# Stores of 64 rows with two adjacent slots, k features by head then slot, batches 1 and 2 transposed on TensorE, and a new step order, in a linear-attention and gated-convolution kernel

## The chip, the cores and the metric

The kernel runs on one core of one Trainium2 chip. The metric is the device time of the launch in microseconds, as a median over several runs. A profile is one execution of its own; its span runs from the first to the last instruction, and its device time lies a little above its span.

## The reference

For each of 8 batches and 8 heads, 576 positions of 64 features go through a linear attention with cosine weights. Its output, with heads side by side as 576 x 512, goes through a projection to three parts, a circular convolution of the second part along the sequence (by FFT), a product of the three and an output projection. All inputs and the output are float32.

```python
def phi(x, c, s):                       # c, s: cos, sin of pi/2 * pos / S
    r = np.maximum(x, 0.0)
    return np.concatenate([r * c, r * s], axis=-1)
q_p, k_p = phi(q, cos_w, sin_w), phi(k, cos_w, sin_w)
kv = np.einsum('bhsf,bhsd->bhfd', k_p, v)
z = np.sum(k_p, axis=2)
num = np.einsum('bhsf,bhfd->bhsd', q_p, kv)
den = np.einsum('bhsf,bhf->bhs', q_p, z)[..., None] + 1e-06
x = (num / den) with heads side by side             # 8 x 576 x 512
proj = x @ w_proj;  x1, x2, x3 = its three parts of 512
x2_conv = irfft(rfft(x2, axis=1) * rfft(filter_fft, axis=0), axis=1)
out = (x1 * x2_conv * x3) @ w_out
```

## The kernel before, in words

**Layout.** The 576 positions of a batch are 64 partitions x 9 consecutive rows. Rows 0 to 4 of each nine stand on partitions 0 to 63 and rows 5 to 8 on partitions 64 to 127, so that a tile of 128 partitions has five "slots" (NJ = 5); slot t holds row t on the lower and row t + 5 on the upper half, and the fifth slot only row 4. This holds for the inputs (load_rows, L260) and for the output rows.

**A batch.** GpSimd's queue loads q, k and v with a cast to fp16 (step_load, L275, "Lq", "Lk", "Lv"); for the first half (4 heads) of batch 0, k and v come over SP's queue as float32 instead (step_load32, "Sk", "Sv", into k32 and v32). VectorE, or ScalarE where the plan's word ends in 'a, makes the features: relu of k ("pk", step_pk, L594) and of q ("pq", L605), a plain relu of all slots and then one scaled relu a slot. k's features lie in `kp` by slot, then head (L196); q's in `qp` by head, then slot. v is scaled by the cosine ("va", L615), and TensorE sums kv over the slots ("kv", L628). q is transposed ("qt", step_qt, L643): for batches from DMA_QT = 1 on by a DMA transpose of two heads on SP's queue, for batch 0 by ten TensorE transposes and one eviction of 128 x 1280. "num" (L664) multiplies it with kv and divides into `att`. `att` is transposed to `xt`: "xt" (L690) is a DMA transpose on SP's queue of two of the four blocks, "xp" (L698) ten TensorE transposes with an eviction of 128 x 1152; batch 0 has "xp", all others "xt". Then come the gates x1 and x3 ("ga", "gb", L830, and their product "g"), the symmetric folding of the sequence ("bf", L709, on VectorE, in halves or whole), the projection x2 ("pr", L742), the forward transform ("dm", "dr", "dl"), the product with the filter's transform ("pd"), the inverse transform ("inv", L865), the unfolding with the gate ("y", L882) and the output ("out", L914).

**Output.** "out" has three groups a batch: slots 0 and 1, slots 2 and 3, and slot 4. For the first two groups one eviction of 128 x 1024 goes to one of three `os` buffers, and SP issues two stores, one for each slot: 128 partitions to the two groups of 64 rows t and t + 5 of each nine (`ov`, L917 and L956). Slot 4 is evicted on 128 partitions as two halves of the columns and stored as two blocks of 64 rows x 256 (L946). In the last batch each slot is evicted in two halves by VectorE and ScalarE and stored alone, the even ones by SP, the odd ones by ScalarE's queue (L959 to L966).

**The order** is written by hand: PLAN (L21) is a list of words, each the next step of a generator, and run (L984) takes them in turn; every instruction enters its engine's or queue's stream in that order. 'v and 'a send an eviction or a relu to VectorE or ScalarE instead of its usual engine; ~ holds a load until the last VectorE instruction issued so far. UNITS (L15) gives the PSUM unit (of four, two banks each) for each use in turn. Some first words are tables: "io" (iotas on GpSimd), "cols", "rows", "tf", "ti", "th", "zero", "pad", "feo", "h" (filter).

Of the kernel before, what the change touches and what calls it, by code (L numbers as in the profile page):

```python
# [15 lines left out]
    "0123013023021032102032102121203031230212030320321320312032021301301231031203123031023103"  # L16
    "2130130202313021302130213013201201230231203120301320312031023021002310123212013213213023"
    "1031202031030120323123031201032020230213203"
# [3 lines left out]
    io:1 io:0 zero: pd32:1 zero: pad:0 pad:5 cols: pad:4 cols: id: rows: io:2 rows: cols:*2 rows:  # L22
    ~Lq:0.0 rows:*5 pd32:0 Sk:0.0 pk:0.0 pk:0.0'a th: pad:1 Sv:0.0 th:'v Lq:0.1 rows:*2 pk:0.0
    va:0.0'v tf:1'v ones:0 pk:0.0'a va:0.0 va:0.0'v*2 pk:0.0'a pk:0.0 warm:0.12 pq:0.0 tf:0'v
    pq:0.0 va:0.0 ones:1 kv:0.0 pq:0.0'a tf:0 pq:0.1 kv:0.0 tf:0 Lv:0.1 Lk:0.1 tf:0 id: pq:0.0
    pq:0.0'a*2 Lv:1.2 qt:0.0 pq:0.1'a*3 th:'v*2 va:0.1'v th: qt:0.1*2 pq:0.1*2 qt:0.2*2 qt:0.0'v
    va:0.1'v pk:0.1 va:0.1 num:0.0 pk:0.1*2 pad:3 io:3 rows: Lw:2.0.4 ~Lw:0.0.4 qt:0.3*2 tf:0
    ~Lk:1.2 pk:0.1 num:0.1 pk:0.1 num:0.1 num:0.0 num:0.1 num:0.0 pk:0.1 pad:2 va:0.1'v*2 Lw:1.0.4
    num:0.1 tf:1 Lq:1.2 kv:0.1*2 num:0.0 num:0.2*2 num:0.3*2 tf:1 num:0.3*2 xp:0.0 num:0.2*2
    xp:0.1 th: xp:0.0'v gb:0.0 bf:0.0 gb:0.1 ga:0.0 bf:0.0 xp:0.1 bf:0.1*3 gb:0.0 gb:0.3 gb:0.0  # L30
    bf:0.0*2 va:1.2'v va:1.2 bf:0.0*2 pk:1.2 rows: tf:1 Lq:2.2 ga:0.0 ga:0.1 bf:0.0 ga:0.1 ga:0.0
    g:0.0 tf:0 ga:0.1 gb:0.1 pk:1.2 bf:0.1*2 pk:1.2 rows: pk:1.2*2 bf:0.1 va:1.2 bf:0.1 gb:0.1
    g:0.1 va:1.2'v tf:1 bf:0.0 pr:0.0 bf:0.1 pr:0.0*2 gb:0.3 gb:0.3'v pq:1.2*4 pr:0.1*3 pq:1.2
    ti:'v ti: va:1.2 pq:1.2 qt:1.0 dm:0.0 pr:0.2*2 pk:1.2 ga:0.2*2 ga:0.2'v ti:*2 gb:0.2 pq:2.2*2
    tf:0 kv:1.2*3 gb:0.2 Lf:1 Lf:0 ti:*2 ga:0.3*2 ga:0.3'v g:0.3 ti: ti:'v dl:0 xe:0.2 gb:0.2
    num:1.0 pq:2.2 num:1.0 pq:2.2'a ~Lv:2.2 dm:0.1 dr:0 qt:1.1 num:1.1 th: feo:1 feo:0 xe:0.0'v
    num:1.0 num:1.1 th: num:1.1 th: num:1.1 qt:1.3 num:1.3*2 h:0 num:1.3*2 num:1.0 xe:0.1 qt:1.2
    ti: num:1.2*2 h:1 num:1.2 g:0.2 num:1.2 h:2 h:0 pd:0.0 pq:2.2*2 va:2.2*2 xt:1.0 gb:1.0 xt:1.1
    pd:0.0 h:2'v va:2.2 Lk:2.2 va:2.2'v qt:2.3 ga:1.1 ga:1.0 h:1 ga:1.2 pd:0.1*2 ga:1.0 pk:2.2
    pd:0.1 ga:1.1 gb:1.0 qt:2.2 ga:1.0 pd:0.0 ga:1.1 pd:0.0 bf:1.2 pk:2.2 pd:0.1 gb:1.2 pd:0.1  # L40
    late: inv:0.1 va:2.2'v gb:1.0 qt:2.1 pk:2.2 pk:2.2'a inv:0.1 gb:1.2 ~Lq:3.2 gb:1.1 bf:1.2
    pk:2.2 bf:1.2 gb:1.1 g:1.0 pk:2.2'a bf:1.2*2 gb:1.1 Lo: gb:1.2 inv:0.0 ga:1.2 inv:0.0 bf:1.2*2
    inv:0.2*2 kv:2.2*2 Lk:3.2 kv:2.2 y:0.4*3 ga:1.2 y:0.4 pr:1.1 inv:0.3*2 y:0.4 num:2.1 num:2.3
    num:2.1 bf:1.2 pq:3.2'a num:2.1*2 num:2.3*2 qt:2.0 pr:1.1 num:2.0 y:0.5 num:2.0*2 pr:1.0*2
    pr:1.1 y:0.5 num:2.0 xt:2.0 num:2.3 pr:1.0 y:0.5 pr:1.2*2 num:2.2*4 pq:3.2 gb:1.3 dm:1.1
    dm:1.0 dr:1 ~Lv:3.2 y:0.5 g:1.2 y:0.5 ga:1.3 gb:1.3 xe:1.1 xe:1.0 pq:3.2*2 dl:1 xe:1.2 pd:1.1
    pq:3.2'a g:1.1 gb:1.3 pd:1.1*2 pk:3.2 ga:1.3 pd:1.1 pd:1.0*2 pd:1.1 va:3.2'v ga:1.3 out:0.1
    gb:2.1 out:0.1 pd:1.0*2 xt:2.1 bf:2.2 va:3.2'v out:0.1 pk:3.2'a*2 ga:2.0 gb:2.0*2 pk:3.2'a
    ga:2.0 pk:3.2 ga:2.0 gb:2.0 out:0.0*2 bf:2.2*2 inv:1.1 out:0.0 Lq:4.2 inv:1.1 pq:3.2'a qt:3.1
    gb:2.1 va:3.2'v g:1.3 gb:2.1 g:2.0 inv:1.0*2 bf:2.2*2 y:1.4*2 inv:1.3 ga:2.2 va:3.2 ga:2.2  # L50
    bf:2.2 ga:2.2 Lv:4.2 bf:2.2 pk:3.2'a inv:1.3 pr:2.0 inv:1.2 pr:2.0 va:4.2'v bf:2.2 out:0.2
    pr:2.2 inv:1.2 pr:2.1*2 va:3.2'v out:0.2 pr:2.0'v out:0.0 qt:3.3 pr:2.2 qt:3.2 y:1.4*2 y:1.5*3
    ~Lk:4.2 kv:3.2 dm:2.0 pq:4.2 kv:3.2 va:4.2*2 pr:2.1 kv:3.2 y:1.5 pq:4.2'a dm:2.1 dr:2 y:1.4
    y:1.5 va:4.2'v Lq:5.2 xe:2.0 pd:2.0 qt:3.0 ga:2.1*3 xe:2.1 num:3.1*3 gb:2.3*2 out:0.2 dl:2
    va:4.2'v ga:2.3 xe:2.2 ga:2.3 pq:4.2'a g:2.1 num:3.1 pq:4.2'a*2 num:3.3 pd:2.0 ga:2.3 gb:2.3
    pd:2.1 num:3.3 pd:2.0 num:3.3*2 pd:2.1*2 out:1.1*3 num:3.0*3 gb:2.2*2 num:3.0 out:1.0 pd:2.1
    out:1.0 num:3.2 pd:2.0 pd:2.1 pk:4.2'a out:1.0 gb:2.2 num:3.2*3 pk:4.2*2 g:2.2 inv:2.3
    inv:2.0*2 pk:4.2 inv:2.3 pq:4.2'a out:1.2 pk:4.2*2 pq:5.2 inv:2.1*2 xt:3.0 g:2.3 y:2.4
    pq:5.2*2 Lk:5.2 inv:2.2*2 y:2.4 kv:4.2*2 pq:5.2 kv:4.2 out:0.2 gb:3.2 gb:3.0 xt:3.1 bf:3.2
    ga:3.0 bf:3.2 qt:4.1 bf:3.2 out:1.2 gb:3.1 ga:3.0*2 gb:3.1*2 qt:4.0 bf:3.2*2 gb:3.0 bf:3.2*2  # L60
    gb:3.0 qt:4.2 gb:3.2 g:3.0 gb:3.2 bf:3.2 num:4.1*2 pk:5.2 ~Lv:5.2 pk:5.2 pr:3.0 num:4.1 pr:3.2
    num:4.0 pr:3.2 num:4.0 pk:5.2 y:2.4 pq:5.2'a num:4.1 qt:4.3 num:4.0 y:2.4*2 pk:5.2'a*2
    pr:3.0*2 ga:3.1*2 num:4.0 ga:3.1 pk:5.2 pr:3.1*3 num:4.2*3 g:3.1 ~Lq:6.2 out:1.0 xt:4.0
    ga:3.2*2 num:4.3 num:4.2 num:4.3 ga:3.2 y:2.5 num:4.3*2 xt:4.1 pq:5.2'a va:5.2'v dm:3.0 dm:3.1
    dr:3 xe:3.0 y:2.5*2 xe:3.1 y:2.5*2 dl:3 pd:3.0 pd:3.1 xe:3.2 out:0.1 pd:3.1*4 gb:3.3*2 ga:3.3
    g:3.2 pq:6.2 ga:3.3 va:5.2 gb:3.3 ga:3.3 gb:4.1 g:3.3 out:2.1*2 ga:4.0 out:2.0 va:5.2 pd:3.0*2
    out:1.2 bf:4.2 out:2.1 pd:3.0 qt:5.3 pq:6.2 out:2.0 bf:4.2*4 qt:5.1 va:5.2*2 ga:4.0*2 ~Lv:6.2
    gb:4.1*2 out:2.0 kv:5.2 gb:4.0 kv:5.2*2 inv:3.2*2 bf:4.2 inv:3.1 inv:3.0 inv:3.1 out:1.2
    num:5.1 inv:3.0 num:5.1*2 Lk:6.2 num:5.1 y:3.4 gb:4.0 num:5.3 pr:4.0 gb:4.0 num:5.3*2 qt:5.0
    num:5.3 out:2.2 num:5.0*3 bf:4.2 pq:6.2'a out:2.2 num:5.0 bf:4.2 pq:6.2'a g:4.0 pr:4.0  # L70
    pq:6.2'a y:3.4 qt:5.2 gb:4.2 pr:4.0 inv:3.3 gb:4.2 inv:3.3 gb:4.2 pq:6.2'a num:5.2*3 ga:4.1
    num:5.2 xt:5.1 ga:4.1 pr:4.2 pr:4.1 ga:4.1 y:3.4*2 y:3.5 va:6.2 y:3.5*2 pr:4.2 g:4.1 out:2.2
    pr:4.1 ga:4.3*2 pr:4.1 dm:4.0 y:3.5 y:3.4 ga:4.3'v dm:4.1 pk:6.2*2 va:6.2 out:2.0 va:6.2 dr:4
    dl:4 y:3.5 gb:4.3 xe:4.2 gb:4.3 ga:4.2 xe:4.0 gb:4.3 pd:4.0 xt:5.0 pk:6.2'a*2 pd:4.0 va:6.2'v
    bf:5.2*4 pk:6.2 xe:4.1 pd:4.1 ga:4.2*2 out:3.1*2 out:3.0*2 gb:5.1 va:6.2 pk:6.2'a g:4.3 pd:4.1
    out:1.1 out:3.0 gb:5.1 out:3.1 pd:4.1 gb:5.1 g:4.2 pd:4.0 kv:6.2*2 ga:5.0 kv:6.2 ~Lq:7.2
    Lk:7.2 pd:4.1*2 pd:4.0 qt:6.2 ga:5.0*2 bf:5.2 inv:4.0*2 qt:6.0 bf:5.2 num:6.0*2 bf:5.2 num:6.0
    bf:5.2 inv:4.1*2 num:6.0 out:2.2 inv:4.2 y:4.4 qt:6.1 y:4.4 num:6.1 y:4.4 num:6.1 inv:4.2
    num:6.1 qt:6.3 pr:5.2 out:3.2 pr:5.2 out:3.2 y:4.4 pr:5.1 num:6.1 out:3.2 inv:4.3*2 pr:5.0
    pq:7.2 num:6.2 num:6.3*4 pr:5.0 Lv:7.2 pr:5.1 pr:5.0 out:3.2 pr:5.1 num:6.2*2 ga:5.1 num:6.2  # L80
    y:4.4 ga:5.1 pk:7.2 ga:5.1 out:3.0 y:4.5*2 dm:5.0 y:4.5*2 dm:5.1 pq:7.2'a y:4.5 xt:6.1 xt:6.0
    dl:5 pk:7.2'a xe:5.2 out:2.1 dr:5 xe:5.0 ga:5.3 pd:5.0*2 gb:5.2 xe:5.1 pd:5.1 gb:5.2 pq:7.2'a
    va:7.2'v ga:5.3 gb:5.0*3 pq:7.2'a*2 out:4.1 g:5.0 gb:5.2 out:4.1 gb:5.3*2 pd:5.1 g:5.1 gb:5.3
    pq:7.2 qt:7.3 pd:5.1*2 pk:7.2 pd:5.1 bf:6.2 pd:5.0*2 bf:6.2*3 va:7.2'v ga:5.3 ga:5.2*3
    va:7.2'v*3 pk:7.2*2 g:5.2 pk:7.2 out:4.0 gb:6.0 out:3.1 out:4.1 out:4.0*2 qt:7.1 g:5.3 inv:5.0
    bf:6.2 inv:5.1 gb:6.0 inv:5.0 inv:5.1 y:5.4 bf:6.2 y:5.4 bf:6.2*2 inv:5.3*2 inv:5.2*2 qt:7.0
    ga:6.0*3 gb:6.0 kv:7.2*2 y:5.4*2 pr:6.0 kv:7.2 num:7.0*2 num:7.1*2 num:7.0 num:7.1 num:7.0
    pr:6.0 pr:6.1 pr:6.0 out:4.1 num:7.3 pr:6.1 num:7.1 num:7.3 pr:6.2 gb:6.1 num:7.3*2 pr:6.2'v
    y:5.4 pr:6.1 out:4.0 qt:7.2 y:5.5*2 gb:6.1*2 dm:6.1 dm:6.0 dl:6 dr:6 y:5.5*2 xe:6.2 out:4.2
    out:4.2'v y:5.5 xe:6.1 gb:6.2*2 pd:6.1 xe:6.0 xt:7.0 num:7.2 ga:6.1 num:7.2*2 out:5.1 num:7.2  # L90
    out:4.2 xt:7.1 pd:6.1*2 g:6.0 ga:6.1*2 ga:6.3*2 g:6.1 ga:6.3 out:5.1*2 gb:6.3 out:5.0*2 pd:6.0
# [14 lines left out]
def kernel(  # L106
# [17 lines left out]
    nc = tc.nc  # L124
# [5 lines left out]
    NJ = 5  # L130
# [899 lines left out]
```

## Time and profile before

| What | us |
|---|---|
| Median of 3 runs (lowest, highest) | 397.08 (394.15, 397.79) |
| The profiled execution's own time | 395.3 |
| Its span | 393.2 |
| TensorE matmul busy | 228.0 |
| TensorE weight load busy (beside matmul) | 141.1 |
| VectorE (DVE) busy | 209.9 |
| ScalarE (ACT) busy | 164.5 |
| GpSimd (POOL) busy | 41.5 |
| Mean granted TensorE clock, share of full speed | 0.776 |
| Bytes read from and written to HBM | 33.69 MB, 9.44 MB |

No engine is busy for more than 58% of the span. The prediction shows the lines of the profile that it draws on. In those, PE is TensorE's matmul, PEld its weight load, SPq the stream of SP, which issues DMAs; "L647" is line 647 of the kernel; a line such as `PE ps L670 <- DMA qpt<-qp: 61.1, 7, 12.2` reads: the matmuls of line 670, which write `ps`, waited for the DMA that writes `qpt` from `qp`, 61.1 us in total in 7 waits, the longest 12.2 us. A helper that issues for many steps (L234, L239, L253) lends its line to all of them, so such rows are told apart by what they read and write.

### The profile page before, as it was taken

To read this page: it belongs to the slowest core of one execution; us is meant where nothing else is said; L and a number is where in the kernel's file an instruction comes from. 1 tells how busy PE (TensorE), PEld (TensorE's weight loads), DVE (VectorE), ACT (ScalarE), POOL (GpSimd) and SP (SyncE) were. 2 spreads that over 40 slices of the span, in tenths; PEclk is the share of its full clock that TensorE was granted. 3 is DMA by queue.
4 is the path that set the end of the run, shared out by engine and by line. 5 is a ranking of instruction groups with operands and counts; after the bars stand their busy time and mean duration, and the time that the engine had idled before them with its cause. 6 is when DMAs were issued, how large, how long until landed. Compare 5 with 4: busy or idle time off the path is not lost.

```text
span 393.2 us, 5622 instructions
## 1 busy us (share of the span) xinstructions
PE 228.0 (58%) x2140; PEld 141.1 (36%) x2140; DVE 209.9 (53%) x618; ACT 164.5 (42%) x252; POOL 41.5 (11%) x78
## 2 busy tenths in 40 slices
PE   4769579899235990451594432994519099970000
PEld 1655447455113750231352312452414056630000
DVE  6889889899223971720292602495206077961000
ACT  3736847789421681142184041390504036530000
POOL 7540203222100020020000300000000000000000
PEclk9569989999866997595598655798667779995555
DMA  8999899999997994999729999199951931111111
GB/s 165 192 202 145 144 192 174 190 173 93 71 159 102 154 113 46 112 68 111 128 49 76 67 112 182 45 90 74 79 89 52 95 66 46 65 38 55 51 63 43
DMA packets 88347, 41.00 MB, mean 104 GB/s; under 512 B 56384, under 2 KB 84032, under 8 KB 88320
## 3 DMA queue, kind: packets, MB, share of 16 engines
q1 hardware_dynamic: 61292, 23.80, 52.3%
q0 software_dynamic: 26688, 16.26, 32.5%
q10 hardware_dynamic: 340, 0.59, 0.4%
q8 instruction: 16, 0.26, 0.3%
q14 instruction: 11, 0.09, 0.1%
HBM read 33.69 MB, written 9.44 MB: 110 GB/s over the span
## 4 chain that ended last, share of the span: by engine, by line
DMA 35%; SPq 21%; PE 20%; DVE 12%; issue 3%; ACT 3%; POOL 1%; DVEq 0%; ACTq 0%
DMA qpt<-qp 16%; SPq L647 11%; PE ps L837 7%; DMA xt<-att 7%; DMA out_dram<-os 6%; SPq L956 5%; DMA raw<-in_q_dram 4%; PE ps L750 3%; PE ps L924 3%; SPq L692 3%; DVE kp L234 2%; DMA raw<-in_v_dram 2%; SPq L946 1%; PE ps L670 1%; DMA att<-in_k_dram 1%
## 5 line engine op out<-in xcount | busy, mean ns | idle before, releaser
L837 PE MATMUL ps<-xt,wp 128*128 128x288 f16 x512 | 79.0, 305 | 33.6 <-DMA xt<-att 26.2
L837 PEld LDWEIGHTS <-wp 128*128 128x128 f16 x512 | 50.8, 103 | 56.3 <-DMA xt<-att 27.6
L239 DVE TENSOR_TENSOR rcp<-ps,epsc 128x10 f32<-128x10 f32 x32 | 5.1, 162 | 97.1 <-PE ps L670 83.4
L670 PE MATMUL ps<-kvs,qpt 128*128 128x65 f16 x320 | 18.3, 217 | 63.5 <-DMA qpt<-qp 61.1
L253 ACT ACTIVATE os<-ps 128x1024 f32<-128x1024 f32 (+1 forms) x20 | 16.5, 833 | 66.2 <-DMA out_dram<-os 32.7
L670 PEld LDWEIGHTS <-qpt 128*128 128x128 f16 x320 | 16.1, 113 | 70.6 <-DMA qpt<-qp 64.9
L750 PE MATMUL ps<-wp,fo 128*128 128x512 f16 x128 | 35.2, 415 | 1.1 <-DVE fo L239 0.7
L924 PE MATMUL ps<-wo,y 128*128 128x512 f16 x128 | 34.4, 415 | 0.0
L253 ACT ACTIVATE x2f<-ps 128x1024 f16<-128x1024 f32 (+1 forms) x21 | 18.5, 898 | 24.5 <-PE ps L750 19.7
L253 ACT CAST x0s<-ps 128x576 f16<-128x576 f32 x28 | 17.8, 639 | 24.8 <-PE ps L837 24.3
L253 ACT CAST x2s<-ps 128x576 f16<-128x576 f32 x31 | 19.6, 640 | 19.6 <-PE ps L837 16.6
L870 PE MATMUL ps<-itab,yf 128*128 128x144 f16 x128 | 20.5, 254 | 11.5 <-ACT os L253 11.3
L239 DVE TENSOR_TENSOR att<-ps,rcp 128x640 f16<-128x640 f32 x32 | 26.0, 821 | 0.5
L253 ACT CAST eq<-ps 128x576 f16<-128x576 f32 x31 | 19.3, 646 | 16.2 <-PE ps L874 16.0
L239 DVE TENSOR_TENSOR eo<-eq 128x512 f16<-128x512 f16 (+1 forms) x72 | 16.4, 284 | 7.6 <-ACT eq L253 7.5
L870 PEld LDWEIGHTS <-yf 128*128 128x128 f16 x128 | 13.8, 112 | 17.7 <-issue 13.1
L239 DVE TENSOR_TENSOR eo<-xt 128x1024 f16<-128x1024 f16 (+3 forms) x36 | 13.6, 418 | 12.3 <-DMA xt<-att 11.2
L874 PE MATMUL ps<-itl,yf 128*128 128x288 f16 x64 | 20.1, 329 | 0.0
L924 PEld LDWEIGHTS <-y 128*128 128x128 f16 x128 | 13.5, 106 | 14.7 <-issue 4.2
L253 ACT CAST xf<-ps 128x1024 f16<-128x1024 f32 (+1 forms) x22 | 16.3, 781 | 5.6 <-PE ps L783 3.6
L635 PE MATMUL ps<-va,kp 128*128 128x65 f16 x320 | 14.1, 200 | 6.8 <-DVE va L351 4.0
L750 PEld LDWEIGHTS <-fo 128*128 128x128 f16 x128 | 12.3, 105 | 15.1 <-issue 5.4
(155 smaller groups left out, 382.8 us busy)
## 6 DMA issues: line engine op xcount, KB each, us to landing
out_dram<-os SPq DMA_DIRECT2D x30, 256.0 KB
raw<-in_v_dram POOLq DMA_DIRECT2D x7, 320.0 KB, 9.0
raw<-in_k_dram POOLq DMA_DIRECT2D x7, 320.0 KB, 13.6
raw<-in_q_dram POOLq DMA_DIRECT2D x7, 320.0 KB, 12.2
raw<-in_v_dram POOLq DMA_DIRECT2D x7, 256.0 KB, 10.6
raw<-in_k_dram POOLq DMA_DIRECT2D x7, 256.0 KB, 15.7
raw<-in_q_dram POOLq DMA_DIRECT2D x7, 256.0 KB, 13.0
wp<-in_moe_w_proj_dram POOLq DMA_DIRECT2D x3, 512.0 KB, 9.8
```

What stands on the lines that cost most here:

```text
L239: last_dve[0] = nc.vector.tensor_tensor(out=out, in0=in0, in1=in1, op=op)
L253: return nc.scalar.copy(out=out, in_=in_) if mul is None else nc.scalar.mul(out=out, in_=in_, mul=mul)
L635: nc.tensor.matmul(u[:, g, ds((h % 4) * 65, 65)], kp[:, j, h].rearrange("p a b -> p (a b)"), va[:, h, j, 0:65], start=(j == 0), stop=(j == ...
L647: nc.sync.dma_start_transpose(out=qpt[:, hsl].rearrange("p h (j n) -> p (h j) n", j=NJ), in_=qp[:, hsl].rearrange("p h j a b -> p (h j a b)"),
L670: nc.tensor.matmul(u[:, hh, ds(t * 65, 65)], qpt[:, h, ds(t * 128, 128)], kvs[:, h // 4, ds((h % 4) * 65, 65)], start=True, stop=True,)
L692: nc.sync.dma_start_transpose(out=xt_buf[b % 2][:, cs].rearrange("p c (t n) -> p (c t) n", t=NJ), in_=att_buf[b % 2][:, cs].rearrange("p c ...
L750: nc.tensor.matmul(u[:, x], fo[:, bl, c, x], wp[c], start=(c == 0), stop=(c == NC - 1),)
L837: nc.tensor.matmul(u[:, hf, 0:HS], wp16[:, i, ds(w * DM + c * 128, 128)], xt[:, i, ds(HS * hf, HS)], start=(i == 0), stop=(i == NC - 1),)
L870: nc.tensor.matmul(u[:, comp, ds(par * QS, QS)], yf[:, comp, ds(par * DM + c * 128, 128)], itab[:, par + 4 * comp], start=(par == 0), stop ...
L874: nc.tensor.matmul(u[:, comp, 0:HS], yf[:, comp, 2 * DM : NF], itl[:, c, comp].rearrange("p a b -> p (a b)"), start=False, stop=True,)
L924: nc.tensor.matmul(u[:, x], y[:, c, ds(128 * t, 128)], wo16[:, c], start=(c == 0), stop=(c == NC - 1),)
L956: nc.sync.dma_start(out=ov[tiles[i]], in_=os_[:, i])
```

## The change

- The first two groups of stores: each of a group's two stores now takes 64 partitions of the `os` buffer, both slots (4 KB a partition), to two adjacent rows of each nine in DRAM (before: 128 partitions, one slot, 2 KB).
- In the last batch each slot is stored in two halves of 64 rows, the lower by SP, the upper by ScalarE's queue.
- `kp` is laid out by head, then slot, and the plain relu walks it in that order.
- DMA_QT is 3: q of batches 1 and 2 is transposed on TensorE; the plan also has "xp" in place of "xt" for these two batches (and "bf" in halves).
- v of batch 0's first half comes by GpSimd's queue as fp16 (V32 = 0) and not by SP's.
- The four small constants are set before the block for the warm-up matmuls; a new step "sine" has ScalarE take one sine of a column into wr_col, which is written again later.
- A new PLAN and a new UNITS (219 uses before, 231 after). In the plan the words change engines in places: 'a on 23 words of pk (16 before) and 10 of pq (25 before); 'v on 4 of qt (1), 23 of va (25).

```diff
-    DMA_QT = 1
+    DMA_QT = 3
+    K32, V32 = 1, 0
...
-    kp_buf = consts_of("kp", 1, [128, NJ, NH, 2, D])
+    kp_buf = consts_of("kp", 1, [128, NH, NJ, 2, D])
...
     def step_zero():
-        nc.vector.memset(warm, 0.0)
-        yield
         nc.vector.memset(half_pi, PI / 2.0)
         nc.vector.memset(m_half_pi, -PI / 2.0)
         nc.vector.memset(m_pi, -PI)
         nc.vector.memset(m_half, -FX / 2.0)
+        yield
+        nc.vector.memset(warm, 0.0)
+        yield
+
+    def step_sine():
+        nc.scalar.activation(out=wr_col, in_=half_pi, func=AF.Sin)
         yield
...
     def step_pk(b, half):
-        rw = k32 if b == 0 and half == 0 else raw_of(b, "k")[:, hs]
-        rj = rw.rearrange("p h (j d) -> p j h d", j=NJ)
+        rw = k32 if b == 0 and half == 0 and K32 else raw_of(b, "k")[:, hs]
+        rj = rw.rearrange("p h (j d) -> p h j d", j=NJ)
-        relu(kp[:, :, hs, 0], rj)
+        relu(kp[:, hs, :, 0], rj)
-            relu(kp[:, j, hs, 1], rj[:, j], tcol[:, j : j + 1])
+            relu(kp[:, hs, j, 1], rj[:, :, j], tcol[:, j : j + 1])
...
-        src = v32 if b == 0 and half == 0 else raw_of(b, "v")[:, hs]
+        src = v32 if b == 0 and half == 0 and V32 else raw_of(b, "v")[:, hs]
...
-                        u[:, g, ds((h % 4) * 65, 65)], kp[:, j, h].rearrange("p a b -> p (a b)"),
+                        u[:, g, ds((h % 4) * 65, 65)], kp[:, h, j].rearrange("p a b -> p (a b)"),
...
     def step_out(b, grp, cut=0):
-        ov = [rows[t : t + 6 : 5] for t in range(4)]
...
             for i in range(2):
-                nc.sync.dma_start(out=ov[tiles[i]], in_=os_[:, i])
+                nc.sync.dma_start(
+                    out=out[b].rearrange("(p j) n -> p j n", j=9)[:, ds(tiles[0] + 5 * i, 2)],
+                    in_=os_[ds(64 * i, 64)],
+                )
...
-            (nc.sync, nc.scalar)[t % 2].dma_start(out=ov[t], in_=os_)
+            nc.sync.dma_start(out=rows[t], in_=os_[0:64])
+            yield
+            nc.scalar.dma_start(out=rows[t + 5], in_=os_[64:128])
             yield
```

Of the plan, the start, the words of batch 1's transposes and the end, before and after:

```diff
-    io:1 io:0 zero: pd32:1 zero: pad:0 pad:5 cols: pad:4 cols: id: rows: io:2 rows: cols:*2 rows:
-    ~Lq:0.0 rows:*5 pd32:0 Sk:0.0 pk:0.0 pk:0.0'a th: pad:1 Sv:0.0 th:'v Lq:0.1 rows:*2 pk:0.0
+    zero: io:1 id: zero: pad:3 io:0 io:2 th: cols: rows: pd32:0 th: rows:*3 pad:0 rows: pad:2
+    pad:1 th:*2 cols: pad:4 warm:0.12 rows:*3 tf:0 rows: id: rows: cols:*2 ones:0 tf:1'v tf:0
+    Sk:0.0 pk:0.0'a tf:1 ones:1 tf:1 pk:0.0'a*2 Lq:0.0 pq:0.0*2 pk:0.0'a*3 tf:0*2 pq:0.0*4 th:
+    Lv:0.0 va:0.0'v qt:0.1 va:0.0'v qt:0.1'v va:0.0'v va:0.0*2 tf:0 qt:0.0 qt:0.0'v Lq:0.1
...
-    ti: num:1.2*2 h:1 num:1.2 g:0.2 num:1.2 h:2 h:0 pd:0.0 pq:2.2*2 va:2.2*2 xt:1.0 gb:1.0 xt:1.1
+    va:2.2*2 num:1.3 num:1.2 pr:0.1 ~Lq:3.2 pr:0.1 feo:0 feo:1 xp:1.0 va:2.2'v*2 h:2 xp:1.0
+    bf:1.0*2 dl:0 xe:0.2 xp:1.1 dm:0.1 dm:0.0 h:2 dr:0 xp:1.1 xe:0.0 pq:2.2 xe:0.1 pq:2.2*3 bf:1.0
...
-    out:7.2.1*2 out:6.1 out:7.1.1*2 out:7.2.1'v out:7.0.1*4 out:7.1.1*4 out:7.2.1*2
+    out:6.0 out:6.1*2 out:7.1.1 out:7.0.1*3 out:7.1.1*2 out:7.2.1*3 out:7.0.1 out:7.1.1*2
+    out:7.2.1*2 out:7.0.1*2 out:7.1.1*2 out:7.0.1 out:7.1.1 out:7.0.1 out:7.1.1
```

## The prediction

> **What bounds the kernel now.** I read the page's 40 slices first, then the waits, then SP's own stream, then a table of stretches. Two lines of the slices, the TensorE clock in tenths of full speed and the busy share of the 16 DMA engines:
>
> ```profile
> PEclk9569989999866997595598655798667779995555
> DMA  8999899999997994999729999199951931111111
> ```
>
> The last seven DMA slices (69 us) stand at 1: one engine in eight, two of sixteen, and in the last four of them the clock has fallen to 5 because nothing is left but stores. Waits over the whole span (us in total, times, longest):
>
> ```profile
> PE ps L670 <- DMA qpt<-qp: 61.1, 7, 12.2
> ACT os L253 <- DMA out_dram<-os: 32.7, 3, 16.2
> PE ps L837 <- DMA xt<-att: 26.2, 4, 15.5
> DVE os L234 <- DMA out_dram<-os: 23.2, 3, 13.8
> ```
>
> TensorE waits for transposed q and transposed attention, and ACT and DVE for a slot of the three `os` buffers, which a store still reads. SP issues both kinds of transfer, in order (start, duration, what):
>
> ```profile
> 39.96 6.14 SPq L647 DMA_TRANSPOSE qpt<-qp  x4
> ...
> 88.27 1.24 SPq L956 DMA_DIRECT2D out_dram<-os  x2
> 89.62 24.82 SPq L647 DMA_TRANSPOSE qpt<-qp  x3
> ```
>
> Four q transposes took 6.14 us to issue before there were stores; three behind the first two stores took 24.82 us. So the stores hold up the transposes behind them. The stretches (window, length, busy time and count of PE, PEld, DVE, ACT, POOL, then clock, DMA share, GB/s):
>
> ```profile
> 0.00:60.00 60.00, 42.78 (x454) 28.37 (x455) 51.31 (x172) 34.70 (x57) 20.06 (x47) 0.83 1.11 173
> 60.00:100.00 40.00, 37.64 (x416) 23.84 (x414) 37.27 (x105) 33.69 (x51) 11.71 (x17) 1.00 1.26 153
> 100.00:122.00 22.00, 3.94 (x22) 1.62 (x20) 3.67 (x9) 5.94 (x7) 0.23 (x1) 0.68 1.32 127
> 122.00:142.00 20.00, 19.14 (x199) 12.70 (x199) 16.64 (x48) 11.53 (x19) 1.36 (x2) 0.93 0.67 112
> 142.00:163.00 21.00, 5.54 (x76) 3.44 (x72) 9.06 (x26) 6.89 (x10) 1.36 (x2) 0.74 1.30 97
> 163.00:191.00 28.00, 11.34 (x95) 7.09 (x96) 5.49 (x12) 6.75 (x10) 2.72 (x4) 0.68 1.24 103
> 191.00:205.00 14.00, 14.00 (x118) 7.97 (x119) 10.52 (x35) 9.61 (x15) 0.00 (x0) 0.80 0.31 61
> 205.00:246.00 41.00, 15.65 (x142) 10.32 (x140) 13.34 (x34) 11.25 (x17) 4.08 (x6) 0.65 1.12 106
> 246.00:262.00 16.00, 15.32 (x139) 8.69 (x140) 10.72 (x26) 9.15 (x14) 0.00 (x0) 0.84 0.63 56
> 262.00:315.00 53.00, 25.94 (x224) 15.41 (x223) 19.78 (x59) 14.25 (x21) 0.00 (x0) 0.75 0.79 82
> 315.00:347.00 32.00, 32.00 (x253) 19.64 (x251) 27.34 (x82) 17.95 (x28) 0.00 (x0) 0.93 0.19 53
> 347.00:393.00 46.00, 4.70 (x28) 2.02 (x25) 4.72 (x18) 2.75 (x6) 0.00 (x0) 0.57 0.15 51
> ```
>
> After 60 us there are two kinds of stretch. In five of them (60-100, 122-142, 191-205, 246-262, 315-347: 122 us) TensorE is fed and is the bound, busy 118.1 of 122 us. In the other six (211 us) everything starves, TensorE busy 67.1 us. In the last, 46 us long, the DMA share is 0.15 and all that moves is stores, at 51 GB/s: a 256 KB store takes 5.1 us, two 10.3 us. 34 such stores make 174 us on two engines that also carry their share of every load and transpose.
>
> **The stores.** A store's DRAM side was 2 groups of 64 rows; it becomes 64 rows of 4 KB, contiguous on both sides, as many bytes in as many instructions (2 a group before the last batch). How many engines the new shape uses no row shows. Bounds: the old rate (51 GB/s, no gain), or all sixteen (an eighth of the time, 0.64 us for 256 KB). The nearest row is the fifth slot's store (L946), 64 rows on both sides: its SP issue at 125.73 us is followed by the next transpose's issue at 128.40, and that lands normally (4.9 us in the chain of waits). In the trace's packet records its 64 packets run up to 16 at a time and are through within 0.55 us, where the 256 KB stores show 2 to 4 at a time. So I take sixteen. Then the `os` waits go, and so does the blockade of the transposes behind a store. What is late next is TensorE itself.
>
> **Fed stretches, 122 us, stay**; two of them run at 0.80 and 0.84 while the clock recovers, at 0.93 their 30 us would be 26.5: 122 - 3 = 119.
>
> **Starved stretches, 211 us, shrink to their TensorE work.** The bounds: 67.1 us as it stands, or, since its mean clock there (weighted by work) is 0.70 against 0.93 when fed, 67.1 x 0.70 / 0.93 = 50.5 us. A window's clock includes its idle time, so some of the work ran warmer: I take 58.
>
> **Transposes of batches 1 and 2 on TensorE.** 8 DMA q transposes and 4 DMA attention transposes leave SP (1.25 to 1.5 us of issue each, and their landings), and 8 x 10 + 4 x 10 = 120 TensorE transposes come. The row:
>
> ```profile
> L656 PE MATMUL ps<-ident,qp 128*128 128x128 f16 x40 | 5.0, 311 | 1.4 <-DVE ident L234 1.1 <-ACT qp L586 0.2
> ```
>
> 5.0 us / 40 = 0.125 us each: 15.0 us, all on the bound engine. They ran at a clock of 0.57; the warm-to-cold ratio of ten L670 matmuls (0.47 to 0.73 us in the timeline) makes it 9.7. I take 12. The Trainium skill, "TensorE: Matmul & The Clock Gate", Part 4, speaks against this: it puts a transpose at about 275 ns in context and says that transposes do not count as activity for the clock. By that page the term would be 120 x 0.275 = 33 us, 21 more than mine. The trace's busy share of 0.125 us contradicts the price; its low clock around transposes (0.50 at 23 to 27 us) does not contradict the rest.
>
> **Other engines.** Evictions: six q evictions on ACT at 1.23 us, two on DVE at 0.82, four attention evictions on ACT at 1.12. Batches 1 and 2 do `bf` in halves, +1.2 us of DVE each (0.42 + 0.18 us twice where 0.69 + 0.22 was once). Eight net relus go from ACT (0.72) to DVE (0.35). The k layout: the full-batch relu of k takes 1.474 us on DVE (x6), the same for q, which has the new layout, 0.817: 6 x 0.66 = 3.9 us less. DVE: 209.9 + 1.6 + 2.4 + 2.8 + 0.8 - 3.9 = 213.6. ACT: 164.5 + 7.4 + 4.5 - 5.8 - 1.2 = 169.4. Both fit beside TensorE (DVE was 84% busy in the fed stretches), so all of this counts 0. Without that cover, +3.7 DVE and +4.9 ACT is the whole price. A wait is added: ACT's q eviction stands until ten transposes are done, with gate evictions queued behind it, for which TensorE's next unit waits; the row for it is 0.8 us in total (ACT qpt <- PE L656, one wait), within the 4 us of waits below. On SP a store still waits in order for its eviction (19.6 us at L946 now) with transposes behind it; the slots come free sooner, so this falls. kv reads each k tile as a 128-wide block as before: 0.
>
> **Start, 0 to 60 us.** v of batch 0 goes from SP (two issues of 0.62 us) to POOL (two of about 0.7), ahead of the second q half on that queue; but q's hold (POOL idle 1.69 us) goes too. ACT waited 1.73 us for v; by POOL's landings of 5.1 us for half batches v comes some 1.4 us later. One 0.27 us memset goes, the sine step adds one small ACT instruction. SP loses two issues of 64. Net 0, bounds -5 to +5: the order is new and I cannot follow every step.
>
> **What remains as waits.** TensorE's idle share in 60-100 us (2.4 of 40, 6%) over the 70 us of new dense work: 4 us. Five batches still use DMA transposes. Bounds per batch: nothing, or the 18.2 us that batch 2 waited at 112 and 122 us beside loads (11.57 + 6.64). The nearest row without a store in the queue is TensorE's waits in the first 100 us, 2.2 us for xt and none for qpt:
>
> ```profile
> PE ps L837 <- DMA xt<-att: 2.2, 1, 2.2
> ```
>
> I take 2.2 x 5 = 11 us.
>
> **Tail.** Now the last multiply of y ends at 349.8 us, 43 us before the end. New: last matmuls 1 us, four tiles and the fifth slot through ACT (5 x 0.38 evicting, 5 x 0.53 to 0.8 issuing, since ACT now issues every second half tile: about 5 us), landing 3 us (estimate, under the 4.7 us of a POOL half load): 9 us, bounds 7 to 13.
>
> **Sum.** 60 + 119 + 58 + 12 + 4 + 11 + 9 = 273 us of span; the profiled execution lies 2.1 us over its span (395.3 to 393.2): 275 us. That execution is 1.8 us under the median of 397.08, which I leave out.
>
> **Rivals.**
> *Transposes collide with loads* instead of stores: batch 2's 18.2 us were waited while three loads of 576 KB moved. Paid in all five batches with nothing to cover it: 5 x (18.2 - 2.2) = 80, so 355; half covered 315. For it: DMA share 1.32 in that window. Against: the first 100 us, as loaded (1.11 to 1.26), cost 2.2. Chance 0.14.
> *The clock does not recover*, because TensorE still pauses between units: 67 instead of 58, 15 instead of 12, no 3 saved: 290; and the 82 fed us after 100 at 0.80 instead of 0.89: 299. For it: 0.80 in 191-205, with TensorE busy throughout. Against: 1.00 in 60-100. Chance 0.12.
> *The stores stay on two engines*: tail and blockades stay, and only the waits of the two batches that leave SP's queue go, 4.9 + 16.7 us (issue and landing of q) and 20.9 (xt) in the chain from 100 and from 142 us: 395 - 42 = 353. The fifth slot's store speaks against it. Chance 0.05.
> *Slower*: the new shape is dealt to fewer engines than now. With one, 34 x 10.3 = 350 us of stores from the first at 88 us on: 438. It decides once a pair takes over (393 - 88) / 17 = 17.9 us against 10.3 now. Chance 0.03.
> Better than all terms, under 256 us (50.5 and 9.7 taken, no waits): 0.04.
>
> **How the numbers follow.** The forecast itself, 275 us, has chance 0.62 and by its bounds 256 to 292. With the clock rival (290 to 299) and the covered edge of the first, about 0.8 lie in 256 to 302. About 1% is what a measurement of this kernel can tell from no change. Every case but the slower one is faster by far more: 0.96 faster, 0.01 within 1%, 0.03 slower.
>
> **What would show it.** Stores: DMA slices of the tail not at 1 for more than a slice, no `os` wait of over 2 us, tail under 13 us from the last y. Transposes: SP's L647 issues all near 1.3 us away from loads. TensorE: over 85% busy from 60 us to the tail, clock 0.9. Layout: the k relu at 0.82 us. Wrong if TensorE shows waits on qpt of over 20 us in total (collision), or a clock under 0.8 with TensorE busy.

## The result, and the profile after

The changed kernel takes 232.38 us (median; 230.7 to 237.1) against 396.16 us for the kernel before: a ratio of 0.585, 95% interval 0.580 to 0.591. The prediction was 275 us with a range of 256 to 302. The direction was right; the kernel is 43 us faster than forecast and 24 us below the range. A single execution is at times a few per cent longer than the others of its kernel (237.1 us here); the ratios leave such executions out, and so do the times of the experiments below, where only experiment 3 shows views of one.

The span of the profiled execution is 228.9 us. The same views as before. First the slices:

```profile
PE   7387899999999999939997999999979999999970
DVE  5999999999999999973988999899999699999860
...
PEclk9859999999999999997999999999999999999996
DMA  6999999999999999999899999999998360601075
```

The long row of ones in the DMA line is gone, and the clock stands at 9 from the fourth slice on but for one slice and the last. TensorE is busy 206.6 us (90% of the span, 58% before), VectorE 203.8, ScalarE 171.5. What TensorE waited for:

```profile
PE ps L844 <- DMA xt<-att: 4.9, 2, 3.6
PE ps L663 <- DVE qp L237: 3.5, 1, 3.5
PE ps L632 <- DVE yf L367: 1.5, 1, 1.5
PE ps L677 <- DVE x2s L254: 1.4, 1, 1.4
```

Line 844 is the gates' line (837 before), 677 that of num (670). The wait for qpt, 61.1 us before, is gone from the matmuls' list (the weight loads wait 2.6 us for it), and the longest wait left is 3.6 us. SP's stream, where three q transposes behind two stores had taken 24.82 us to issue:

```profile
85.84 5.57 SPq L654 DMA_TRANSPOSE qpt<-qp  x3
91.51 1.17 SPq L962 DMA_DIRECT2D out_dram<-os  x2
92.78 4.64 SPq L699 DMA_TRANSPOSE xt<-att  x2
```

Two transposes behind two stores now issue in 4.64 us. The stretches (columns as before):

```profile
0.00:60.00 60.00, 52.01 (x674) 37.70 (x675) 56.44 (x201) 52.43 (x84) 30.62 (x62) 0.94 1.17 171
60.00:100.00 40.00, 37.99 (x441) 24.19 (x438) 39.34 (x122) 36.55 (x56) 5.57 (x8) 1.00 1.20 178
100.00:120.00 20.00, 18.41 (x198) 12.44 (x199) 13.99 (x45) 12.28 (x20) 2.73 (x4) 0.91 1.09 183
120.00:140.00 20.00, 18.58 (x176) 13.58 (x175) 18.83 (x46) 14.64 (x22) 3.32 (x4) 1.00 1.17 188
140.00:160.00 20.00, 19.24 (x213) 11.08 (x212) 18.46 (x56) 16.57 (x24) 1.37 (x2) 1.00 1.23 198
160.00:180.00 20.00, 18.67 (x208) 12.52 (x207) 17.60 (x50) 13.16 (x20) 0.00 (x0) 1.00 1.02 188
180.00:200.00 20.00, 20.00 (x185) 12.23 (x184) 18.81 (x49) 11.05 (x16) 0.00 (x0) 1.00 0.36 84
200.00:215.00 15.00, 15.00 (x141) 9.04 (x139) 13.94 (x47) 9.95 (x15) 0.00 (x0) 1.00 0.08 21
215.00:229.00 14.00, 6.68 (x41) 3.15 (x38) 6.41 (x28) 4.82 (x9) 0.00 (x0) 0.86 0.58 163
```

No starved stretch is left. TensorE's idle time, window less busy, is 8.0 us in the first 60, 2.0 to 100, 5.1 to 215 and 7.3 in the tail: 22.4 us in all, and the span is that plus the 206.6 busy.

### The profile page after: what moved, and what is told of

The parts are those of the page before. It is cut to its first block, busy times and chain, and to the rows that moved or that the text cites. A ratio compares the mean times of both kernels' runs of the same rounds, so it can differ in the third digit from the quotient of the medians.

```text
span 228.9 us, 5857 instructions
## 1 busy us (share of the span) xinstructions
PE 206.6 (90%) x2260; PEld 135.9 (59%) x2260; DVE 203.8 (89%) x637; ACT 171.5 (75%) x261; POOL 43.6 (19%) x80
## 5 line engine op out<-in xcount | busy, mean ns | idle before, releaser
L844 PE MATMUL ps<-xt,wp 128*128 128x288 f16 x512 | 73.6, 290 | 5.8 <-DMA xt<-att 4.9
L757 PE MATMUL ps<-wp,fo 128*128 128x512 f16 x128 | 31.2, 379 | 0.4 <-ACT os L256 0.4
L930 PE MATMUL ps<-wo,y 128*128 128x512 f16 x128 | 30.6, 379 | 0.0
L256 ACT CAST x0s<-ps 128x576 f16<-128x576 f32 x29 | 18.7, 649 | 10.6 <-PE ps L844 10.0
L242 DVE TENSOR_TENSOR att<-ps,rcp 128x640 f16<-128x640 f32 x32 | 25.9, 820 | 0.5
L242 DVE TENSOR_TENSOR g<-x0s,x2s 128x576 f16<-128x576 f16 x32 | 14.3, 451 | 4.4 <-ACT x2s L256 3.8
L877 PE MATMUL ps<-itab,yf 128*128 128x144 f16 x128 | 16.7, 226 | 0.0
L881 PE MATMUL ps<-itl,yf 128*128 128x288 f16 x64 | 16.6, 286 | 0.0
L242 DVE TENSOR_TENSOR y<-eo 128x512 f16<-128x512 f16 (+1 forms) x72 | 16.3, 283 | 0.0
L242 DVE TENSOR_TENSOR eo<-xt 128x512 f16<-128x512 f16 (+3 forms) x44 | 14.6, 367 | 1.7 <-DMA xt<-att 1.7
L677 PE MATMUL ps<-kvs,qpt 128*128 128x65 f16 x320 | 14.2, 197 | 1.9 <-DVE x2s L254 1.4
L465 ACT ACTIVATE va<-raw,ccol 128x512 f16<-128x512 f16 (+1 forms) x22 | 14.6, 697 | 1.4 <-DMA raw<-in_v_dram 1.4
## 6 DMA issues: line engine op xcount, KB each, us to landing
wp<-in_moe_w_proj_dram POOLq DMA_DIRECT2D x3, 512.0 KB, 10.2
```

Source lines behind the costliest of these rows:

```text
L242: last_dve[0] = nc.vector.tensor_tensor(out=out, in0=in0, in1=in1, op=op)
L256: return nc.scalar.copy(out=out, in_=in_) if mul is None else nc.scalar.mul(out=out, in_=in_, mul=mul)
L465: return nc.scalar.activation(out=dst, in_=src, func=AF.Copy if bias is None else AF.Identity, scale=col, **({} if bias is None else {"bia ...
L677: nc.tensor.matmul(u[:, hh, ds(t * 65, 65)], qpt[:, h, ds(t * 128, 128)], kvs[:, h // 4, ds((h % 4) * 65, 65)], start=True, stop=True,)
L757: nc.tensor.matmul(u[:, x], fo[:, bl, c, x], wp[c], start=(c == 0), stop=(c == NC - 1),)
L844: nc.tensor.matmul(u[:, hf, 0:HS], wp16[:, i, ds(w * DM + c * 128, 128)], xt[:, i, ds(HS * hf, HS)], start=(i == 0), stop=(i == NC - 1),)
```

## The experiments

Theory A: the old stores, on two engines, starved the kernel, and the rest of the change is small. Theory B: half of the gain comes from the TensorE transposes and the new order.

**1. The new stores alone in the kernel before** (old plan, DMA transposes from batch 1 on, old k layout)

```diff
-                nc.sync.dma_start(out=ov[tiles[i]], in_=os_[:, i])
+                nc.sync.dma_start(
+                    out=out[b].rearrange("(p j) n -> p j n", j=9)[:, ds(tiles[0] + 5 * i, 2)],
+                    in_=os_[ds(64 * i, 64)],
+                )
...
-            (nc.sync, nc.scalar)[t % 2].dma_start(out=ov[t], in_=os_)
+            nc.sync.dma_start(out=rows[t], in_=os_[0:64])
+            nc.scalar.dma_start(out=rows[t + 5], in_=os_[64:128])
```

> The kernel before with the new stores alone (old plan, DMA transposes from batch 1 on, old k layout). Theory A (the two store engines caused the starving and the cold clock; the rest of the change is small): the tail falls from 46 to about 10 us, TensorE is busy about 204 us (228 less the 24 to 28 us that a warm clock is worth), its idle 17 us in the first 60 us and some 30 us behind: 245 to 262 us. Theory B (the transposes on TensorE and the new order bring half of it; DMA transposes beside loads keep TensorE waiting 15 to 18 us in each of several batches): 290 to 330 us.

Measured: 250.4 us, ratio 0.633 (0.621 to 0.644), span 249.5, clock 0.926. Its page and TensorE's waits:

```profile
PE 208.6 (84%) x2140; PEld 132.1 (53%) x2140; DVE 209.7 (84%) x618; ACT 163.4 (66%) x252; POOL 41.3 (17%) x78
```

```profile
PE ps L670 <- DMA qpt<-qp: 7.8, 4, 2.9
PE ps L837 <- DMA xt<-att: 5.3, 3, 3.3
```

This lies in theory A's range. The very instructions that were busy 228.0 us on TensorE are busy 208.6 us, and the waits for the two kinds of transposes fall from 87 to 13 us. By themselves the stores take off 146 us (396.7 to 250.4, beside this run), where the whole change takes off 164.

**2. The changed kernel with the old stores**

```diff
-                nc.sync.dma_start(
-                    out=out[b].rearrange("(p j) n -> p j n", j=9)[:, ds(tiles[0] + 5 * i, 2)],
-                    in_=os_[ds(64 * i, 64)],
-                )
+                nc.sync.dma_start(out=ov[tiles[i]], in_=os_[:, i])
...
-            nc.sync.dma_start(out=rows[t], in_=os_[0:64])
-            yield
-            nc.scalar.dma_start(out=rows[t + 5], in_=os_[64:128])
+            (nc.sync, nc.scalar)[t % 2].dma_start(out=ov[t], in_=os_)
+            yield
```

> The changed kernel with the old stores (128 partitions, one slot, two groups of 64 rows), all else new. Theory A: 34 stores of 256 KB at 5.14 us are 175 us on two engines from about 91 us on, at least 266 us, and the transposes of batches 3 to 7 stand behind them again: 310 to 370 us. Theory B: the new order covers most of it, and only the stores themselves set the end: 266 to 285 us.

Measured: 345.9 us, ratio 0.874 (0.860 to 0.888). Its last stretches and a wait:

```profile
220.00:260.00 40.00, 19.39 (x190) 12.21 (x191) 14.67 (x43) 10.31 (x16) 0.00 (x0) 0.70 0.81 95
260.00:300.00 40.00, 34.02 (x269) 19.96 (x268) 28.99 (x88) 19.67 (x28) 0.00 (x0) 0.91 0.23 56
300.00:344.00 44.00, 4.09 (x25) 1.75 (x23) 3.83 (x15) 2.83 (x6) 0.00 (x0) 0.59 0.14 51
```

```profile
PE ps L844 <- DMA xt<-att: 40.4, 4, 18.5
```

The starved stretches, the cold clock and the tail at a DMA share of 0.14 and 51 GB/s are back: theory A's range again, from the other side. But the rest of the change is not small: with the old stores it takes off 51 us (396.7 to 345.9). Alone, the two parts take off 146 and 51 us, together 164: some 33 us are such as either part removes.

**3. The changed kernel with the transposes of batches 1 and 2 by DMA**

```diff
-    DMA_QT = 3
+    DMA_QT = 1
...
     def step_xp(b, x):
+        if b > 0:
+            opened[0] += 1
+            yield from step_xt(b, x)
+            yield
+            return
         u = unit16()
```

(step_qt likewise passes over its PSUM unit and its second step for batches 1 and 2, so that the order of everything else stays.)

> The changed kernel with q and the attention of batches 1 and 2 transposed by DMA as before (120 TensorE transposes and 12 evictions fewer). Theory A: TensorE loses 120 x 0.082 = 10 us of work, but the first 100 us are full of loads (DMA share 1.2), so some transposes land late: -5 to +10 us against the changed kernel, 226 to 242 us. Theory B: each of the two batches pays up to 18 us of waits: 250 to 270 us.

Measured: 274.8 us; the views are of the other execution, of 284.2 us. Theory A's upper end of 242 us missed by over 30, and even theory B's 270 was passed: in the new order it matters a great deal where these transposes run. SP's stream and TensorE's in that stretch:

```profile
22.51 26.67 SPq L656 DMA_TRANSPOSE qpt<-qp  x4
```

```profile
46.87 0.73 PE L681 MATMUL ps<-kvs,qpt 128*128 128x65 f16 x10 [8.59 <-DMA qpt<-qp]
56.99 0.73 PE L681 MATMUL ps<-kvs,qpt 128*128 128x65 f16 x10 [9.39 <-DMA qpt<-qp]
```

The new order begins batch 1 at 22 us, when GpSimd is still issuing loads (until 37.5 us; DMA share 1.38 from 20 to 40 us). Four DMA transposes that issue in 6.1 us where no load had been issued for 14 us (at 40 us in the kernel before) take 26.7 there, and TensorE, which takes its matmuls in order, stands at num. Experiment 7, with batch 1 alone by DMA, has the same: 25.92 us for these four, and 18.2 us of waits for qpt in the first 60 us.

**4. The changed kernel with the old stores in the last batch only**

```diff
-            nc.sync.dma_start(out=rows[t], in_=os_[0:64])
-            yield
-            nc.scalar.dma_start(out=rows[t + 5], in_=os_[64:128])
+            (nc.sync, nc.scalar)[t % 2].dma_start(out=ov[t], in_=os_)
+            yield
             yield
```

> The changed kernel with the old stores in the last batch's four slots only. Both theories put these four stores of 256 KB on two engines: 4 x 5.14 = 20.6 us from the first issue at about 221 us: end at 243 to 246 us of span against 228.9, 245 to 249 us of time. If two stores on two queues ran on different engines, it would be 235.

Measured: 249.3 us, span 247.5 (the other execution 253.3). From the first issue at 222.3 us it is 25 us to the end, in which these four stores and the fifth slot's move at 52 GB/s:

```profile
222.33:247.50 25.17, 0.08 (x2) 0.00 (x0) 0.85 (x2) 1.42 (x4) 0.00 (x0) 0.55 0.17 52
```

So the form of four stores is worth some 18 us at the end of the kernel (231.7 to 249.3), where nothing covers it, and two issuing queues do not help: in the trace's packet records the four stores run two packets at a time for both queues together. In the kernel before, the first two of the old stores, from SP alone, run two at a time as well, 512 KB in 10.75 us, which is 49 GB/s.

**5. The new stores and the TensorE transposes in the old order**

```diff
     def step_qt(b, hp):
...
+        if b >= 1:
+            u = spare()
+            for hh in range(2):
+                for j in range(NJ):
+                    nc.tensor.transpose(u[:, hh, ds(j * 128, 128)], ..., ident)
+            ev(qpt[:, hsl], u[:, :, 0:SP_])
+            yield
+            return
```

(for batches 1 and 2, and the same for the attention; spare() takes a PSUM unit that no open step holds; one word of the plan, qt:2.2, goes one place later.)

> The kernel before (old order, old k layout) with the new stores, and with q and the attention of batches 1 and 2 transposed on TensorE, each in one step with its eviction on ScalarE. Against the stores alone (249.5 us of span): if the TensorE transposes gain by themselves, by taking those batches off the DMA engines, 235 to 243. If they gain only because the new order uses them to begin batch 1 earlier, TensorE pays about 10 us for 120 transposes and gets back some 4 us of waits: 248 to 258.

Measured: 274.6 us (the other execution 278.8), 24 us slower than the stores alone and far beyond both ranges. TensorE's busy time is 223.2 us and its idle time 49.7, against 208.6 and 40.9 in experiment 1: of 23.4 us more of span 14.6 are busy time, 10.2 of them the 120 new transposes (7.3 us for q, 2.9 for the attention), and 8.8 are idle. A part of the chain of waits:

```profile
52.86 0.68 PE ps L670 x10
53.56 1.23 ACT qpt L266
...
56.81 1.21 ACT qpt L266
58.07 0.73 PE ps L694 x10
58.80 2.56 PE ps L573 x6
61.36 1.08 PE ps L670 x10
62.46 1.23 ACT qpt L266
63.74 0.73 PE ps L694 x10
```

Ten transposes, their eviction on ScalarE and ten matmuls of num (L694) stand one behind the other on the path, with only six matmuls of the filter (L573) between one num and the next transposes. I read this so: an order laid out for a transfer that runs by itself leaves little other work between a transpose and its use. Put into the old order in this way, each in one step with its eviction, the transposes gain nothing. The loads of later batches, which wait for buffers, also came late (a DMA share of 0.34 in 60 to 100 us); how much of the loss is each was not separated.

**6 and 7. Only batch 2, or only batch 1, by DMA in the changed kernel** (experiment 3 with `b == 2` or `b == 1` alone)

> The changed kernel with only batch 2's q and attention by DMA. If the loss seen with both batches by DMA (279 against 232) came from transposes meeting the loads of the first 65 us, batch 2, whose transposes come at about 65 to 85 us, costs little: 229 to 240. If the new order has no room for any DMA transpose, about half the loss: 250 to 258.

> The changed kernel with only batch 1's q and attention by DMA. Loads of the first 65 us as the cause: nearly the whole loss, 262 to 282. No room anywhere: half of it, 250 to 258.

Measured: 257.9 us with batch 2 by DMA, 263.6 with batch 1. These two runs can't tell the cases of the expectation apart. It took batch 2's transposes to come at 65 to 85 us, but its four q transposes came at 47.9 us, beside loads that GpSimd issued from 42.3 to 58.6 us, and took 12.9 us to issue. So both batches met loads, and their losses of 26 and 32 us are more together than the 43 us of both at once. In both kernels one wait for qpt stands out, of 13.0 and of 10.6 us:

```profile
PE ps L681 <- DMA qpt<-qp: 19.0, 5, 13.0
```

(of the kernel with batch 2 by DMA). About half of the 26 us is that wait. Much of the rest came later: from 60 to 100 us TensorE idles 17.6 us, against 2.0 in the changed kernel. That loads of the next batches were held up behind the delayed work fits (GpSimd's longest wait before a load is 37.6 us there, 18.5 in the changed kernel), but no run isolates it.

**8. Stores of 64 rows with one slot each**

```diff
-            for i in range(2):
+            for i in range(4):
                 nc.sync.dma_start(
-                    out=out[b].rearrange("(p j) n -> p j n", j=9)[:, ds(tiles[0] + 5 * i, 2)],
-                    in_=os_[ds(64 * i, 64)],
+                    out=rows[tiles[i // 2] + 5 * (i % 2)], in_=os_[ds(64 * (i % 2), 64), i // 2],
                 )
```

> The changed kernel with four stores of 64 rows and one slot (2 KB pieces) for each group in place of two with two slots (4 KB); the last batch as it is. If the 64 rows are what spreads a store over the engines, the only cost is 28 more SP issues of 0.55 us, spread over 130 us: 230 to 238. If the 4 KB pieces matter, the stores take about twice as long to land and the transposes behind them too: 240 to 260.

Measured: 237.4 us, ratio 0.600 (0.587 to 0.614). The 64 rows do nearly all; two slots in one store, which halve SP's issues, are worth some 5 us, with intervals that still touch (0.580 to 0.591 for the changed kernel). A store lands 2.4 us after its issue here (median; a store of the first two groups is 128 KB), against 3.4 in the changed kernel (256 KB). From 203 us on the packet records show 13 of its 2 KB packets at a time, where the old stores with the same 2 KB show two; TensorE waits 8.2 us for qpt. Not separated is whether it was the two groups of 64 rows on the DRAM side or the 128 partitions that kept an old store on two engines.

**9 to 12. Four small ones side by side**

The changed kernel again; the old k layout in it; v of batch 0 by SP as float32 (`V32 = 1`, its "pad" word and "Sv" in place of "Lv" in the plan); and all stores of the fifth slot from ScalarE's queue (`nc.scalar.dma_start`).

> The changed kernel once more, as the measure for the three beside it: 230 to 234 us.

> The changed kernel with k's features by slot, then head, as before. The plain relu of k then takes 1.47 in place of 0.82 us on VectorE in six batches, 3.9 us in all. If TensorE is the only bound (VectorE busy 89%, each relu with room before it): 0 to +1.5 us. If VectorE bounds as well: +3 to +5 us.

> The changed kernel with v of batch 0's first half over SP's queue as float32 again. My prediction priced this part at 0, bounds -5 to +5. If v is not what the start waits for: -1 to +1 us. If the start waits for v's landing on POOL's queue (some 1.4 us later by my estimate): -1 to -3 us; if the float32 reads cost more on VectorE and ScalarE than the landing: +1 to +3.

> The changed kernel with all stores of the fifth slot issued from ScalarE's queue, which also evicts them: 14 issues of 0.6 us fewer on SP ahead of transposes, 8.4 us more issuing on ScalarE (busy 75%). If TensorE's last DMA waits (7.5 us for xt and qpt) come from SP's queue being full, as the 28 further issues of the one-slot stores suggest (+5 us): -1 to -4 us. If they come from the transposes' own landing, 0; if ScalarE has no room, +1 to +4.

Measured, as ratios to the kernel before: 0.587 (0.584 to 0.591), 0.591 (0.587 to 0.595), 0.585 (0.582 to 0.589), 0.594 (0.592 to 0.597); in us 231.3, 233.8, 230.1, 234.6. The k layout and v's queue can't be told from nothing; the relu itself is as predicted, here with the old layout:

```profile
L237 DVE TENSOR_SCALAR kp<-raw 128x2560 f16<-128x2560 f16 x6 | 8.9, 1477 | 0.0
```

against 4.9 us (816 ns each) in the changed kernel. ScalarE as issuer of the fifth slot's stores (15 issues moved, not 14) is slower by about 3 us. That is the expectation's case of a ScalarE without room; which wait it came from was not shown. None of these is clearly faster than the changed kernel.

## Why the prediction was right or wrong

**The stores: right.** "So I take sixteen" holds (experiments 1, 2, 4): in the packet records of the changed kernel four stores issued from 195 us on run 14 packets at a time on average, where the old ones run two. One size was off: a 256 KB store was to take 0.64 us, an eighth of the old time. These four move 1 MB in 4.1 us, 1.0 us a store, a fifth. The last 12 us of the changed kernel, in which stores are all that moves, with pauses between them (a DMA share of 0.67):

```profile
217.00:228.90 11.90, 4.68 (x28) 2.02 (x25) 4.43 (x16) 3.31 (x8) 0.00 (x0) 0.84 0.67 188
```

188 GB/s is 3.7 times the old 51, not 8 times. It costs little, since TensorE is the bound until the tail. A smaller slip: the old kernel has 32 such stores (30 from SP, 2 from ScalarE), not the "34" of the prediction, so that they make 165 us and not 174; this touches the slower rival and not the forecast.

**The two halves of the error.** By the prediction's own sum, the stores without TensorE transposes would have been 273 - 12 us of span, and 2.2 us more for each of two more batches with DMA transposes: 265. Experiment 1 gives 249.5. From there the prediction adds 8 for the transposes and nothing for order, layout and start; measured from experiment 1 to the changed kernel are -20.6 us. So 16 of the 44 us of error lie in the stores' part and 28 in the rest. By terms, of 273 us against 228.9: 21 us are TensorE's busy time, 9 its idle time in the first 60 us, 12 the later waits and 2 the rest.

**"Starved stretches shrink to their TensorE work ... I take 58", "122 - 3": mis-sized.** The prediction's sum holds 228 us of TensorE busy time; it is 206.6. This is the term that failed most: I took the middle between a cold and a warm reading; the warm end was nearer, and even that was too cold, because I left the first 60 us and the fed stretches nearly as they were. The gates' and num's matmuls in the three kernels (before, stores alone, after):

```profile
L837 PE MATMUL ps<-xt,wp 128*128 128x288 f16 x512 | 79.0, 305 | 33.6 <-DMA xt<-att 26.2 <-ACT os L253 7.4
L670 PE MATMUL ps<-kvs,qpt 128*128 128x65 f16 x320 | 18.3, 217 | 63.5 <-DMA qpt<-qp 61.1 <-DVE xf L251 1.5 <-ACT kvs L253 0.5
```

```profile
L837 PE MATMUL ps<-xt,wp 128*128 128x288 f16 x512 | 74.9, 294 | 6.3 <-DMA xt<-att 5.3 <-ACT os L253 0.9
L670 PE MATMUL ps<-kvs,qpt 128*128 128x65 f16 x320 | 15.9, 202 | 10.5 <-DMA qpt<-qp 7.8 <-DVE xf L251 1.5 <-ACT kvs L253 0.5
```

```profile
L844 PE MATMUL ps<-xt,wp 128*128 128x288 f16 x512 | 73.6, 290 | 5.8 <-DMA xt<-att 4.9 <-ACT xt L256 0.4 <-DVE xt L254 0.4
L677 PE MATMUL ps<-kvs,qpt 128*128 128x65 f16 x320 | 14.2, 197 | 1.9 <-DVE x2s L254 1.4 <-ACT kvs L256 0.5
```

The same 512 matmuls fall from 79.0 to 73.6 us, the 320 of num from 18.3 to 14.2, as the mean clock goes from 0.776 over 0.926 to 0.969. Without all transposes (7.5 us before, 14.7 after) TensorE's busy time falls by 220.5 - 191.9 = 28.6 us, where the sum had 12 (3 and 9). The clock rival (290 to 299) went the wrong way altogether.

**"I take 12" for the transposes: too dear, and the skill's price further off.** The row's 120 now:

```profile
L663 PE MATMUL ps<-ident,qp 128*128 128x128 f16 x120 | 10.2, 241 | 3.8 <-DVE qp L237 3.5 <-ACT qp L593 0.4
```

0.085 us each with the cold ones of batch 0, 0.072 in a warm run of ten. The 80 new ones of q take 5.9 us, the 40 of the attention 2.9: 8.8 us for all 120. (TensorE's transposes in all go from 7.5 to 14.7 us, since those of batch 0 now run warmer.) By the Trainium skill's page "TensorE: Matmul & The Clock Gate", Part 4, the estimate was 120 x 0.275 = 33 us, and the page has transposes not counted as activity for the clock. Here the clock is 1.00 in 20 to 30 and 40 to 60 us, with 80 q transposes among 425 matmuls, so a few transposes between matmuls do not cool it. What transposes alone would do, no run here shows.

**"Start ... Net 0, bounds -5 to +5": failed.** TensorE idles 8.0 us in the first 60 where it idled 17.2 (16.6 in experiment 1): -9, and it does more of the later work there (52.0 us busy, 42.8 before). The step that I passed over is that transposes on TensorE let batch 1 begin at 22 us, among the loads, where its first DMA transpose had been issued at 40 us; I priced them as work taken off SP and put on TensorE, and not by what they let start. With batch 1 by DMA (experiment 7) TensorE is busy 33.0 us in the first 60, against 52.0.

**"What remains as waits", 15 us: mis-sized.** Between 60 us and the tail TensorE idles 7.1 us in all; the prediction had 4 + 11 and, in its fed stretches, 3.9. The old order has 15.7 (experiment 1), so there the estimate was sound. What removed the rest is the new order with its transposes on TensorE; which words of the order do it was not tested. The rival of transposes that collide with loads was a true danger: it is what experiments 3, 6 and 7 show, at 26 to 43 us, but only for transposes that the change had moved away from the loads.

**Right:** the tail (9 us forecast; 9.1 from the last multiply at 219.8 us to the end), and the other engines counted as covered (VectorE 203.8 us, ScalarE 171.5; the forecast's 213.6 and 169.4 have VectorE too high by 10, of which I looked for no cause). VectorE, at 89%, is now nearly as full as TensorE.

**The range.** Its low end was too high by its own terms: with all lower bounds (start -5, starved work 50.5, transposes 9.7, no waits, tail 7) the span was about 241 us and the time 243, and I cut at 256. The measured time lies under even that: no case allowed for an order that fits the new transfers.

## What to carry to other kernels

Where the DMA share stands at a small fixed fraction while the kernel waits for transfers, look at how the slow transfer is shared among the engines before anything else; here stores on two engines held up the transposes behind them in SP's queue, and the lost time came back a second time as a cold TensorE clock (228.0 us busy against 208.6 for the same instructions). When such a blockade goes, price all of TensorE's work at the clock of its best stretch, not only the starved part. And price a step that moves between engines by what it lets begin or makes wait in the given order: the same TensorE transposes cost 24 us in one order and saved 43 in the other (experiments 5 and 3). With the new stores, the old order takes 250.4 us with DMA transposes and 274.6 with TensorE's, the new order 274.8 and 231.7: each half of the step alone loses, and both together gain.

## What the runs showed of the hardware that was not expected

- Spreading the stores gave 188 GB/s against 51 in the last microseconds, and 1 MB in 4.1 us where four follow each other closely, not the eight times of sixteen engines for two. A store lands 3.4 us after its issue with 256 KB in 4 KB pieces, 2.4 us with 128 KB in 2 KB pieces (medians).
- DMA transposes beside loads: four took 26.7, 25.9 and 12.9 us to issue among loads (experiments 3, 7 and 6), 6.1 us at 40 us in the kernel before, where no load had been issued for 14 us.
- Stores of the old form issued from two queues ran no faster than from one (52 GB/s in experiment 4, 49 for the first two in the kernel before).
